# A gated delta-rule kernel: chain matmuls on four array tiles, part of the convolution on TensorE, and a new schedule

## The chip, the cores and the metric

The kernel runs on one core of one Trainium2 chip. The metric is the device time of one execution in microseconds (us). Engines are named as in the profile: PE is TensorE (PEld its weight loads), DVE is VectorE, ACT is ScalarE, POOL is GpSimd, SP is the SyncE queue from which all transfers are issued.

## The reference

There are two parts. The first is a delta-rule recurrence over 768 tokens for 4 batches x 8 heads of width 48, the second a gated convolution block on the result (model width 384, kernel of 5 taps). Cut to what matters:

```python
k_n = k / (norm(k) + 1e-6)
state = zeros(B, H, 48, 48)
for t in range(768):
    y[t] = q[t] @ state
    state += beta[t] * outer(k_n[t], v[t] - k_n[t] @ state)
x = y as [B, S, 384]
gate_pre[s] = sum(conv_w[j] * x[s - 4 + j] for j in range(5))
out = (sigmoid(gate_pre) * (x @ w_val)) @ w_out
```

All values are fp32. The three weights arrive as 64-bit numbers and are turned into fp32 on the chip.

## The kernel before

The tokens are cut into 12 chunks of 64. Within a chunk the recurrence becomes matrix work: with L the masked, scaled matrix of key products of the chunk, one needs the inverse T of a unit triangular 64 x 64 matrix for each of the 32 (batch, head) pairs; then u = T (v - k S), S += k^T u and y = q S + (q k^T masked) u. Heads come in pairs: a state of two heads lies in partitions 0 to 47 and 64 to 111.

Two chunks form a group; there are six groups. The work of a group (`prep`):

- `gram` (L455, or `gram0` L465 for group 0): key and query products, through PSUM into GL by ACT. Group 1 to 5 multiply against block-diagonal keys that are loaded a second time (KBD).
- `diag` (L473, L474) and a 32 x 32 transpose (L478) put the diagonal 32 x 32 blocks of all heads along the free axis, so that DVE can invert them all at once, one partition per row of work. `coef` (L414 to L443) makes the norms by a root iteration.
- The inverse of 32 x 32 blocks: `row` up to 8 (L498, L500), `mergez8` and `merget8` to 16 (L508 to L523), `zmul`, `zred`, `tmul`, `tred` to 32 (L527 to L547). The largest multiplies of the last stage run on POOL (buffers D and PR2), the others on DVE. Two transposes (L552, L554) bring the blocks back.
- `lev1` and `lev2` (L564, L585) join two 32-blocks to a 64-block on PE in 32 x 32 array tiles; ACT copies around them fill BD (`bdcopy` L575).
- `vscale` (L449, POOL) scales the values, `att` (L682, POOL) masks the query products into AQ.

The work of a chunk (`chain`) is done in two halves of 8 head pairs: `emul` (v - kS, as one matmul with the identity stacked under the keys), `umul` (L713), `smul` (L725, L727, accumulated in PSUM), `ymul` (L739, L741), each with an ACT copy out of PSUM. y comes out feature-major; a copy and twelve small SP transfers per chunk (X<-YS) put it into the layout of the second part.

The second part of a chunk (`moe`): for each of three blocks of 128 features, the five taps on [128, 4 x 64] tiles (one ACT copy, `tap` L783 on DVE, one product on ACT added by POOL, L790), the sigmoid (L793), `val` (L798, PE), `gate` (L802, DVE); then `outp` (L809), `oevac` and four stores.

No order is written by hand. Each piece is put into a planner (`Plan`) with an engine, a cost in us and its inputs and outputs; the planner simulates the engines with these costs, a rank (longest path plus a table of biases, BIAS), and gives one order of emission. It also inserts matmuls on zeros (`keep_warm`, L853) where it finds PE idle or thinly loaded.

Of the kernel before, what the change touches and what calls it, by code (L numbers as in the profile page):

```python
# [27 lines left out]
BIAS = {
    'GVH': 49.4, 'GVL': 430.5, 'LB': -960.7, 'LF': 103.3, 'LK': 1063.7, 'LQ': 47.2, 'LV': -635.0, 'Lk0K': 76.9,
    'Lk0Q': -227.5, 'Lkt': 472.7, 'Lo': 12.9, 'Lw': 61.8, 'Lx': 463.6, 'WH': 5.2, 'WL': -222.6, 'XL': 23.3,  # L30
    'att': -654.8, 'bdcopy': 453.2, 'blankB': -14.6, 'blankK': -5.4, 'blankQ': 209.3, 'blankU': -168.4, 'coef': -53.2,
    'conv': -269.0, 'cscale': -35.7, 'diag': -136.2, 'eevac': -29.7, 'emul': -281.2, 'eye': -11.2, 'eyes': 10.6,
    'f64c': 43.2, 'f64cj': 4.7, 'f64cl': 14.4, 'f64o': 61.4, 'f64oj': -34.2, 'f64ol': -83.4, 'f64v': -24.1,
    'f64vl': -54.5, 'fill': 2.2, 'gate': 102.4, 'gevac': -110.2, 'gevac0': 63.3, 'gram': -91.8, 'lev1': -38.0,
    'lev2': 175.8, 'masks': -18.5, 'merget8': 176.4, 'mergez8': -6.7, 'norm_red': -132.3, 'norm_sq': 5.7,
    'outp': 647.7, 'sevac': 334.2, 'sig': -447.3, 'smul': 978.1, 'tap': -856.6, 'tap_product': -1442.2,
    'tap_sum': 526.0, 'tevac': -12.4, 'tmul': -23.0, 'trans_in': 80.0, 'trans_out': 92.7, 'tred': 22.8,
    'uevac': 251.2, 'umul': 622.2, 'val': -383.5, 'vscale': -451.5, 'yevac': 75.3, 'ymul': -21.4, 'zevac': 7.1,
    'zmul': -1217.5, 'zred': -24.9, ('GVH', 0): -59.0, ('GVH', 1): -430.0, ('GVH', 5): 228.9, ('GVL', 1): 101.2,
# [5 lines left out]
    ('att', 0): -27.8, ('att', 1): 1.5, ('att', 5): 6.3, ('bdcopy', 0): 29.7, ('bdcopy', 1): -449.2,  # L45
    ('bdcopy', 5): -329.1, ('blankB', 0): 39.8, ('blankK', 0): -125.7, ('blankQ', 0): 8.4, ('blankU', 0): 68.6,
    ('coef', 0): 14.0, ('coef', 1): 141.0, ('coef', 5): 81.4, ('conv', 0): -53.4, ('conv', 1): -178.5,
    ('conv', 5): 33.1, ('cscale', 0): 4.7, ('cscale', 1): 12.2, ('cscale', 5): 15.9, ('diag', 0): 23.4,
    ('diag', 5): 333.9, ('eevac', 0): 15.5, ('eevac', 1): 80.1, ('eevac', 5): -272.3, ('emul', 1): -1.5,
    ('emul', 5): -5.0, ('eye', 0): 64.3, ('eyes', 0): -3.8, ('f64c', 0): 269.1, ('f64cj', 0): -81.2,  # L50
    ('f64cl', 0): -55.7, ('f64o', 0): -13.4, ('f64oj', 0): -87.5, ('f64ol', 0): 82.9, ('f64vj', 0): 372.9,
    ('f64vl', 0): -98.5, ('fill', 0): -18.9, ('gate', 1): -126.5, ('gate', 5): 236.8, ('gevac', 1): -23.1,
    ('gevac', 5): -92.7, ('gevac0', 0): -365.9, ('gram', 1): -331.6, ('gram', 5): -0.7, ('gram0', 0): 27.8,
    ('halo', 0): 15.7, ('halo', 1): -217.4, ('halo', 5): -331.7, ('lev1', 0): 101.2, ('lev1', 1): 149.0,
    ('lev1', 5): 88.8, ('lev2', 0): 4.1, ('lev2', 1): -57.3, ('lev2', 5): 32.6, ('masks', 0): 209.6,
    ('merget8', 0): 210.5, ('merget8', 1): 72.8, ('merget8', 5): 0.3, ('mergez8', 0): -5.5, ('mergez8', 1): 49.0,
    ('mergez8', 5): 281.0, ('norm_red', 0): -83.0, ('norm_sq', 0): -51.1, ('oevac', 0): -199.0, ('oevac', 1): 169.8,
    ('oevac', 5): -211.1, ('outp', 0): -232.0, ('outp', 1): 40.4, ('row', 0): 14.6, ('sevac', 0): -94.5,
    ('sevac', 1): -307.3, ('sevac', 5): -11.7, ('sig', 0): 5.8, ('sig', 1): -5.8, ('sig', 5): 354.3,
    ('smul', 0): -154.9, ('smul', 1): 128.2, ('smul', 5): -91.0, ('tap', 0): -120.7, ('tap', 1): 22.3,  # L60
    ('tap', 5): 46.7, ('tap_product', 0): -49.4, ('tap_product', 1): -8.8, ('tap_product', 5): 227.5,
    ('tap_sum', 0): -106.3, ('tap_sum', 1): 160.8, ('tap_sum', 5): -86.9, ('tevac', 0): -222.2, ('tevac', 1): -300.8,
    ('tevac', 5): 27.0, ('tmul', 0): -55.3, ('tmul', 1): 203.6, ('tmul', 5): -0.8, ('trans_in', 0): -3.8,
    ('trans_in', 1): -3.0, ('trans_in', 5): -27.1, ('trans_out', 5): 52.7, ('tred', 0): -66.1, ('tred', 1): 89.7,
    ('tred', 5): -16.7, ('uevac', 0): 113.1, ('uevac', 1): 29.9, ('uevac', 5): -10.0, ('umul', 0): -192.2,
    ('umul', 1): -4.4, ('umul', 5): 78.7, ('val', 0): -30.2, ('val', 1): -4.4, ('val', 5): -12.8,
    ('vscale', 0): -102.0, ('vscale', 5): 87.3, ('yevac', 0): 9.1, ('yevac', 1): 136.9, ('yevac', 5): 24.2,
    ('ymul', 0): -3.0, ('ymul', 1): -22.7, ('zevac', 1): 187.4, ('zevac', 5): -1.7, ('zmul', 1): -228.0,
    ('zmul', 5): 72.0, ('zred', 1): 74.8, ('zred', 5): -18.6,
# [11 lines left out]
class Plan:  # L81

    HOP = {"PE": 0.2, "ACT": 0.2, "DVE": 0.12, "POOL": 0.15, "SP": 1.6}  # L90

    def __init__(self, slots, bias):
        self.bias, self.part, self.kinds = bias, 0, []
        self.ops, self.writer, self.readers, self.slots = [], {}, {}, dict(slots)
        self.load = {}

    def pe(self, t, cost, cols):


        part = 0.0  # L100
        while part < 1.0:
            k = int(t / TICK + 1e-9)
            rate = (1.0 if self.load.get(k - 1, 0.0) >= TICK_COLS else 0.5) / cost
            dt = min((1.0 - part) / rate, TICK * (k + 1) - t)
            self.load[k] = self.load.get(k, 0.0) + cols * dt * rate
            part, t = part + dt * rate + 1e-9, t + dt
        return t

    def add(self, eng, cost, fn, args=(), r=(), w=(), take=None, give=None, cols=0, kind=None):
# [818 lines left out]
```

## Time and profile before

| what | value |
|---|---|
| three runs | 412.46 us median (411.55 to 415.64) |
| profiled execution, span | 416.2 us |
| mean granted TensorE clock | 0.881 |
| PE, PEld | 352.4 us, 297.6 us busy |
| DVE, ACT, POOL | 324.6, 233.7, 172.4 us busy |
| PE instructions | 5836 matmuls, 5836 weight loads |
| filler matmuls (L853) | 416 of these, 62.6 us |
| moved by transfers | 45.31 MB, 109 GB/s |

A group line of the profile reads: line, engine, operation, output<-inputs, shapes, count, then busy us, mean ns of one, and the idle time before them with what ended it. The mean of one matmul contains its way through the array, so the busy us divided by the count, or the distance of the starts, is what one costs in a row of many. A windows line reads: stretch, its length, then busy us (and instructions) of PE, PEld, DVE, ACT and POOL, granted clock, DMA share, GB/s.

### The profile page before, as it was taken

How to read it: one execution, taken by the hardware profiler on the slowest of the kernel's cores; microseconds unless marked ns; L12 is line 12 of the kernel's file. 1: busy time of each engine (PE TensorE's matmuls, PEld its weight loads, DVE VectorE, ACT ScalarE, POOL GpSimd, SP SyncE). 2: the span in 40 equal slices, each digit the busy share in tenths (PEclk: the TensorE clock that was granted, in tenths of full speed). 3: DMA queues.
4: the chain of work that ended last, by engine and by line, in shares of the span. 5: the costliest groups of instructions: out<-in, count | busy, mean ns of one | idle time of the engine just before them, and what ended most of it. 6: DMA issues, size and time to landing. Idle time of an engine off the chain costs nothing.

```text
span 416.2 us, 13720 instructions
## 1 busy us (share of the span) xinstructions
PE 352.4 (85%) x5836; PEld 297.6 (71%) x5836; DVE 324.6 (78%) x576; ACT 233.7 (56%) x509; POOL 172.4 (41%) x138
## 2 busy tenths in 40 slices
PE   8849967997499969989798999597599793999995
PEld 6849967886398738767586877476578593878883
DVE  5689999998894998988988379989587999320550
ACT  8403327966386636957377765353777364876420
POOL 4263650837802727505663233557023477100200
...
GB/s 222 166 251 198 157 183 50 145 151 192 52 151 116 142 14 157 104 122 139 154 106 157 128 130 142 106 61 131 49 2 79 78 114 24 2 41 13 48 39 38
DMA packets 59805, 45.31 MB, mean 109 GB/s; under 512 B 44576, under 2 KB 47776, under 8 KB 59744
## 3 DMA queue, kind: packets, MB, share of 16 engines
...
q8 instruction: 46, 0.75, 0.8%
q14 instruction: 15, 0.12, 0.1%
...
## 4 chain that ended last, share of the span: by engine, by line
PE 52%; DVE 21%; DMA 11%; issue 6%; ACT 4%; SPq 3%; POOL 2%; DVEq 0%; POOLq 0%; ACTq 0%
PE gram L455 9%; PE SPS L853 9%; PE val L798 9%; PE out L809 8%; DVE GT L783 6%; PE u L713 4%; SPq L304 3%; DVE TTR L552 2%; DMA GL<-in_kq_dram 2%; PE SPS L725 2%; DMA AQ<-in_conv_w_dram 2%; PE z L564 2%; DVE TT__85 L547 2%; PE gram L465 2%; DVE PR L508 2%
## 5 line engine op out<-in xcount | busy, mean ns | idle before, releaser
L783 DVE SCALAR_TENSOR_TENSOR GT<-X,CW,GT 128x256 f32<-128x256 f32 x111 | 73.1, 684 | 12.9 <-POOL GT L790 12.2
L790 POOL TENSOR_TENSOR GT<-GT,TP 128x256 f32<-128x256 f32 x33 | 27.0, 817 | 97.7 <-ACT TP L299 97.4
L853 PE MATMUL SPS<-ZW 128*128 128x128 f32 x416 | 62.6, 309 | 0.0
L853 PEld LDWEIGHTS SPS<-ZW 128*128 128x128 f32 x416 | 58.5, 220 | 2.7 <-issue 1.0
L798 PE MATMUL val<-X,WV 128*128 128x256 f32 x216 | 58.9, 415 | 1.0 <-ACT BD L299 1.0
L809 PE MATMUL out<-WO,GT 128*128 128x384 f32 x144 | 52.1, 511 | 6.8 <-DVE GT L802 6.7
L455 PE MATMUL gram<-KQ,KBD 96*128 96x128 f32 x320 | 54.5, 331 | 0.8 <-DMA KQ<-in_kq_dram 0.8
L455 PEld LDWEIGHTS gram<-KQ,KBD 96*128 96x128 f32 x320 | 49.0, 237 | 2.3 <-ACT BD L299 0.9
L798 PEld LDWEIGHTS val<-X,WV 128*128 128x128 f32 x216 | 41.2, 203 | 7.6 <-ACT BD L299 1.1
L802 DVE TENSOR_TENSOR GT<-val,GT 128x256 f32<-128x256 f32 x36 | 15.0, 420 | 39.4 <-PE val L798 32.7
L575 ACT ACTIVATE BD<-TTR 32x512 f32<-32x512 f32 x48 | 30.1, 628 | 27.2 <-DVE TTR L552 26.7
L809 PEld LDWEIGHTS out<-WO,GT 128*128 128x128 f32 x144 | 27.4, 198 | 24.6 <-DVE GT L802 7.7
L449 POOL TENSOR_TENSOR US<-VT,NRM 64x768 f32<-64x768 f32 x24 | 36.4, 1516 | 19.7 <-DMA VT<-in_vt_dram 10.7
L299 ACT ACTIVATE GL<-gram 128x512 f32<-128x512 f32 x48 | 27.9, 594 | 23.4 <-PE gram L455 15.9
L793 ACT ACTIVATE GT<-GT 128x256 f32<-128x256 f32 x36 | 14.7, 415 | 43.4 <-DVE GT L783 43.1
L564 PE MATMUL z<-TTR,GL 32*32 32x32 f32 x768 | 12.0, 210 | 29.8 <-DVE TTR L552 21.6
L682 POOL TENSOR_SCALAR_AFFINE_SELECT AQ<-GL 64x1024 f32<-64x1024 f32 x24 | 28.7, 1195 | 15.4 <-PE y L739 8.9
L564 PEld LDWEIGHTS z<-TTR,GL 32*32 32x32 f32 x768 | 9.6, 123 | 34.0 <-DVE TTR L552 15.5
L713 PEld LDWEIGHTS u<-VT,BD 128*64 128x64 f32 x704 | 26.4, 157 | 9.5 <-ACT BD L299 4.5
L713 PE MATMUL u<-VT,BD 128*64 128x48 f32 x704 | 29.0, 242 | 4.5 <-ACT BD L299 3.6
L739 PE MATMUL y<-AQ,US 112*64 112x64 f32 x384 | 28.2, 226 | 1.8 <-ACT X L299 1.8
L299 ACT ACTIVATE OS<-out 128x384 f32<-128x384 f32 x24 | 11.8, 490 | 30.4 <-PE out L809 26.7
...
## 6 DMA issues: line engine op xcount, KB each, us to landing
...
```

Source lines behind the costliest of these rows:

```text
L299: A.activation(out=out, in_=in_, func=AF.Copy, **kw)
L449: G.tensor_tensor(out=USV[(2 * g + c) % 3][r, a], in0=VT[c][r].rearrange("p (h n) d -> p h n d", h=2), in1=n.unsqueeze(3).to_broadcast([64 ...
L455: PE.matmul(p[:, 128 * j:128 * (j + 1)], KBD[h % 2][:, j, :], KQ[h % 2][:, j, :], start=True, stop=True)
L564: PE.matmul(p[to:to + 32, x:x + 32], GL[r + 32:r + 64, u, 0:32], TTR[r + 32:r + 64, u, :], start=True, stop=True, tile_position=(r + 32, to))
L575: A.activation(out=BD[c][q:q + 32, :, q:q + 32], in_=TTR[q:q + 32, u0:u0 + NP, :], func=AF.Copy)
L682: G.affine_select(out=AQ[c][r0:r0 + 64, :, j, :], in_=GL[r0:r0 + 64, c * NP:(c + 1) * NP, 64:128], pattern=[[0, NP], [1, C]], compare_op=A ...
L713: PE.matmul(p[64 * a:64 * a + 64, D * j:D * j + D], BD[c][:, h * HB + j, 64 * a:64 * a + 64], VT[c][:, h * HB + j, :] if ch else us[:, a, ...
L739: PE.matmul(p[0:64, C * j:C * j + C], US[ch % 3][0:112, 0, h, D * j:D * j + 64], AQ[c][0:112, pp, 0, :], start=True, stop=True)
L783: eng.scalar_tensor_tensor(out=GT[m], in0=x[:, m, :, k:k + C], scalar=CW[:, m, k:k + 1], in1=GT[m], op0=ALU.mult, op1=ALU.add)
L798: PE.matmul(p[:, 0:B * C].rearrange("p (b t) -> p b t", t=C), WV[:, k, 128 * m:128 * m + 128], xs[:, k], start=(k == 0), stop=(k == NKT - 1))
L809: PE.matmul(bank["o", ch, i][:, 0:DM], GT[k][:, 2 * i:2 * i + 2, :].rearrange("p b t -> p (b t)"), WO[:, k, :], start=(k == 0), stop=(k == ...
L853: PE.matmul(SPS[0][:, 384:512], ZW, ZW, start=False, stop=True, skip_group_check=True)
```

## The change

The kernel is rewritten around the same algorithm.

- **Pairing.** Partitions 0 to 63 and 64 to 127 now hold tokens of different batches (two streams t, two halves r). Every step of the chain is 32 matmuls of 48 columns, each on one 64 x 64 tile of the array: four tiles in turn (`STREAMS`) in `estep`, `qstep`, `sstep`, `ystep`, two in `ustep`. The subtraction of the values is a DVE operation (`esum`); the part of y from the state (`qstep`) is a step of its own that is accumulated in PSUM with `ystep`.
- **One gram.** Keys and queries of a chunk come in one load KQ (two transfers of 480 KB). `gram` makes 32-token blocks on 64 x 32 tiles, 64 matmuls of 96 columns per chunk; ACT copies the key blocks (`gk`), DVE multiplies the query blocks with a mask (`ga`). `att`, `diag`, KBD and KQ0 go.
- **Inverse.** The 8 and 16 stages are as before. In groups 1 to 5 all multiplies of the last stage are on DVE. In group 0 (`FAST`) the 16 to 32 stage is done by PE and ACT instead (`pack`, `trans_x`, `split`, `p1`, `wsum`, `p2`, `p3`). `bd0`, `zevac`, `tevac` copy on ACT.
- **Values** are scaled on ACT, head by head (16 copies of 48 columns per chunk).
- **y** is token-major; `flip` transposes it on PE against an identity, ACT copies it into X. The twelve transfers go.
- **Taps.** Three of five taps are matmuls with diagonal weights (`conv`, 9 matmuls of 256 columns per chunk), the other two stay on DVE, the first of them reading PSUM. The ACT copy and the POOL addition go.
- **Banks.** PSUM is two banks for the states and six that any piece may take.
- **Schedule.** New costs, ranks and biases in the planner, and a term by which PE gets at most 256 instructions in 3.6 us. Filler is placed by the same kind of rule.

The core of the diff, with the parts that do this (removed functions are named above):

```diff
+SUPPLY = 3.6
+BLOCK = 256
-DENSE = (6.722264986890762e+22, 1800.0, 1300.0)
+DENSE = 600.0
...
+    STREAMS = ((0, 0), (1, 1), (0, 1), (1, 0))
+    def gram(c, i, part):
+        x = KQ[c % NKQ]
+        for j in range(4):
+            h = 4 * i + j
+            for k in range(2):
+                for r, t in STREAMS:
+                    q = 64 * t + 32 * k
...
+                    PE.matmul(o, w, y, start=True, stop=True, tile_position=(64 * r, q))
...
+        if g in FAST:
+            for b in range(2):
+                add("ACT", 0.5, pack, (b,), r=["TT"], w=["PR"])
+            add("DVE", 0.63, trans_x, w=["PR"])
+            add("ACT", 1.15, split, (1,), r=["PR", "MHI"], w=["RH"])
+            add("ACT", 1.15, split, (0,), r=["PR", "TRQ"], w=["TZ"])
...
+        else:
+            for kb in range(4):
+                add("DVE", 0.06 + 64 * (16 - 4 * kb) / 960.0, zmul, (kb,), r=["TL", "TT"], w=["PR"])
+                add("DVE", 0.07 + 64 * (16 - 4 * kb) / 960.0, zred, (kb,), r=["PR"], w=["ZT"])
...
+        def estep():
+            for h in range(H):
+                for r, t in STREAMS:
+                    PE.matmul(bank("e", c, r)[64 * t:64 * t + C, D * h:D * h + D], x[64 * r:64 * r + D, t ^ r, h, 2 * T:4 * T],
+                              sp[64 * r:64 * r + D, t ^ r, h, :], start=True, stop=True, tile_position=(64 * r, 64 * t))
+        def esum(r):
+            V.tensor_tensor(out=ES[:, r], in0=vw(bank("e", c, r)), in1=vn[:, r], op=ALU.subtract)
+        def ustep():
+            for h in range(H):
+                for r in range(2):
+                    for t in (0, 64):
+                        PE.matmul(bank("u", c, r)[t:t + C, D * h:D * h + D], bd[t:t + C, u0 + 8 * r + h, :],
+                                  (ES if c else vn)[t:t + C, r, h, :], start=True, stop=True, tile_position=(t, t))
+        def sstep():
+            for h in range(H):
+                for r, t in STREAMS:
+                    PE.matmul(SPS[t ^ r][64 * r:64 * r + D, D * h:D * h + D], kt_[64 * t:64 * t + C, r, h, :],
+                              us[64 * t:64 * t + C, r, h, :], start=False, stop=True, skip_group_check=True,
+                              tile_position=(64 * t, 64 * r))
...
+        def flip(r):
+            p = bank("x", c, r)
+            for i in range(NKX):
+                PE.transpose(p[:, 128 * i:128 * i + 128], YS[r][c % 2][:, 128 * i:128 * i + 128], EYE)
...
         def conv(m):
-            copy(A, GT[m], x[:, m, :, 0:C], scale=CW[:, m, 0:1])
+            p = bank("c", c, m)[:, 0:B * C].rearrange("p (b t) -> p b t", t=C)
+            for k in range(nt):
+                PE.matmul(p, CD[:, m, k], x[:, m, :, k:k + C], start=(k == 0), stop=(k == nt - 1))
+        def tap(m, k):
+            V.scalar_tensor_tensor(out=GT[m], in0=x[:, m, :, k:k + C], scalar=CW[:, m, k:k + 1],
+                                   in1=csum(m) if k == nt else GT[m], op0=ALU.mult, op1=ALU.add)
```

More of the change, by code (lines that the diff above doesn't have):

```diff
@@ L17 @@
 B, H, S, D = 4, 8, 768, 48
-C = 64
-NG = S // (2 * C)
-NP = 16
+T = 32
+C = 2 * T
+NC = S // C
+NG = NC // 2
 NU = 32
-HB = 8
-QB = 4
+KW = 5 * T
 DM = H * D
-NKT = DM // 128
+NKX = DM // 128
 KS = 5
-WAIT = {"PE": (0, 0), "ACT": (0.25, 0.5), "DVE": (0, 0), "POOL": (0.4, 0.8), "SP": (0.3, 0)}
+NBANK = 6
 BIAS = {
[L29 to L39, printed above, removed]
[5 rows of a table removed]
[L45 to L69, printed above, removed]
-}
@@ L90, with __init__, add @@
     HOP = {"PE": 0.2, "ACT": 0.2, "DVE": 0.12, "POOL": 0.15, "SP": 1.6}
[L92 to L109, printed above, removed]
+    def __init__(self, bias):
+        self.bias, self.part = bias, 0
+        self.ops, self.kinds, self.writer, self.readers = [], [], {}, {}
+        self.bank = {}
+    def add(self, eng, cost, fn, args=(), r=(), w=(), take=(), give=(), cols=0, size=0, kind=None):
         n = len(self.ops)
@@ L207, in forward @@
                 done = free[e] + self.HOP[e]
-            if give:
-                slots[give].append(done)
+            for key in give:
+                banks.append((done, self.where[key]))
             ready[e].remove(n)
@@ L215, in forward @@
                     ready[ops[u][0]].append(u)
+        self.span = max(free.values())
         return start, fill
@@ new lines, with bank, copy @@
+    MHI = sb.tile([128, 1], F32, name="MHI")
+    M0 = sb.tile([128, 1], F32, name="M0")
+    MLO = TRQ[:, 16:17]
+    ZW = sb.tile([128, 128], F32, name="ZW")
+    SPS = [ps.tile([128, 512], F32, name=f"SPS{i}") for i in range(2)]
+    PB = [ps.tile([128, 512], F32, name=f"PB{i}") for i in range(NBANK)]
+    plan = Plan(BIAS)
+    add = plan.add
+    def bank(*key):
+        return PB[plan.where[key]]
+    dma = lambda kb: kb / 230.0
+    def copy(out, in_, **kw):
+        A.activation(out=out, in_=in_, func=AF.Copy, **kw)
@@ new lines, in trans_x, with split, p1 @@
+        def trans_x():
+            V.transpose(out=TX, in_=XL)
+        def split(hi):
+            if hi:
+                copy(RH, TX.rearrange("p j u -> p u j"), scale=MHI[:, 0:1])
+            else:
+                copy(TZ[:, :, 0:16], TX.rearrange("p j u -> p u j"), scale=MLO)
+        def p1(i):
+            for j in range(16):
+                for q in (0, 64, 32, 96):
+                    PE.matmul(bank("w", g, i)[q:q + 32, 16 * j:16 * j + 16], GD[gb][q:q + 32, 16 * i + j, T:],
+                              RH[q:q + 32, 16 * i + j, :], start=True, stop=True, tile_position=(q, q))
@@ L840 @@
-    plan.add("SP", dma(98), load, (BE, beta), w=["BE"], kind="LB")
-    for i in range(1 + 2 * NKT):
-        plan_weights(i)
+            copy(OS[2 * (c % 2) + i], bank("o", c, i)[:, 0:DM])
+        X_ = [("X", c % 3, 0), ("X", c % 3, 1)]
+        if not last:
+            add("POOL", 0.3, halo, r=X_, w=[("Xh", (c + 1) % 3)])
+        for m in range(NKX):
+            gt = ("GT", c % 2, m)
+            add("PE", 0.47 * nt, conv, (m,), cols=512 * nt, size=4 * nt, r=X_ + [("Xh", c % 3), ("CD", m)], w=[("cp", c, m)],
+                take=[("c", c, m)])
+            for k in range(nt, KS):
+                add("DVE", 0.4, tap, (m, k), r=X_ + [("Xh", c % 3), "CW"] + ([("cp", c, m)] if k == nt else []), w=[gt],
+                    give=[("c", c, m)] if k == nt else ())
+            add("ACT", 0.36, sig, (m,), r=[("cp", c, m)] if nt == KS else [], w=[gt], give=[("c", c, m)] if nt == KS else ())
+            add("PE", 1.3, val, (m,), cols=1536, r=X_ + [("W", i) for i in range(1, NKX + 1)], w=[("vp", c, m)],
+                take=[("v", c, m)], size=12)
+            add("DVE", 0.34, gate, (m,), r=[("vp", c, m)], w=[gt], give=[("v", c, m)])
```

1003 lines of the change are left out of this document (500 added, 503 removed), and 15 rows, old and new, of the table BIAS.

## The prediction

> **What bounds the kernel now.** I read the busy shares first, then the chain, the stretches of 10 us, and the waits.
>
> ```profile
> span 416.2 us, 13720 instructions
> PE 352.4 (85%) x5836; PEld 297.6 (71%) x5836; DVE 324.6 (78%) x576; ACT 233.7 (56%) x509; POOL 172.4 (41%) x138
> ...
> PE 52%; DVE 21%; DMA 11%; issue 6%; ACT 4%; SPq 3%; POOL 2%; DVEq 0%; POOLq 0%; ACTq 0%
> ...
> L853 PE MATMUL SPS<-ZW 128*128 128x128 f32 x416 | 62.6, 309 | 0.0
> ```
>
> PE looks like the bound, but L853 is the filler that keeps its clock up. Without it PE works 352.4 - 62.6 = 290 us, less than DVE's 324.6. The stretches show who waits:
>
> ```profile
> 100.00:110.00 10.00, 1.60 (x36) 1.22 (x33) 8.61 (x8) 0.89 (x2) 9.26 (x6) 0.64 0.63 117
> 110.00:120.00 10.00, 9.74 (x159) 8.81 (x159) 9.72 (x18) 9.50 (x18) 3.24 (x3) 0.50 0.62 130
> ...
> 340.00:350.00 10.00, 3.26 (x25) 2.96 (x23) 9.89 (x9) 2.08 (x5) 9.85 (x8) 0.93 0.19 33
> ...
> 370.00:380.00 10.00, 9.92 (x287) 8.77 (x275) 1.17 (x3) 6.63 (x18) 0.00 (x0) 1.00 0.11 25
> ```
>
> The columns are PE, PEld, DVE, ACT and POOL busy, granted clock, DMA share. Once per group (at 100, 340) PE starves while DVE and POOL finish the block inverse, and at 110 the clock it then gets is 0.50. After 350 the last inverse is done, DVE has 1.17 of 10 us to do and PE alone works off what is left.
>
> ```profile
> PE z L564 <- DVE TTR L552: 21.6, 3, 8.2
> ```
>
> So DVE's inverses set the pace up to 350, PE the last 66 us. The profiled execution (416.2 us) lies just above the three runs (411.55 to 415.64, median 412.46): I count 0.99 of the span as the time.
>
> **DVE.** Much of its time is waiting beside POOL. These rows are taps without and with a POOL multiply (263.27 to 267.78) beside them, and the same L540 multiply both ways:
>
> ```profile
> 150.42 1.26 DVE L783 SCALAR_TENSOR_TENSOR GT<-X,CW,GT 128x256 f32<-128x256 f32 x3
> 263.83 5.02 DVE L783 SCALAR_TENSOR_TENSOR GT<-X,CW,GT 128x256 f32<-128x256 f32 x4
> ```
> ```profile
> 265.23 2.55 POOL L527 TENSOR_TENSOR D<-TLP,TT__85 128x1024 f32<-128x1024 f32 x1
> ```
> ```profile
> 55.57 1.04 DVE L540 TENSOR_TENSOR PR<-ZT,TT__85 128x512 f32<-128x512 f32 x1
> ...
> 57.51 1.86 DVE L540 TENSOR_TENSOR PR<-ZT,TT__85 128x768 f32<-128x768 f32 x1
> ```
> ```profile
> 101.67 2.44 DVE L540 TENSOR_TENSOR PR<-ZT,TT__85 128x512 f32<-128x512 f32 x1
> ```
>
> 0.42 us a tap alone, 1.25 beside POOL; 1.04 against 2.44. The change empties POOL (only halo, weights and masks stay), so the short values hold. The other terms:
>
> ```profile
> L783 DVE SCALAR_TENSOR_TENSOR GT<-X,CW,GT 128x256 f32<-128x256 f32 x111 | 73.1, 684 | 12.9 <-POOL GT L790 12.2
> L802 DVE TENSOR_TENSOR GT<-val,GT 128x256 f32<-128x256 f32 x36 | 15.0, 420 | 39.4 <-PE val L798 32.7 <-ACT BD L299 5.6 <-ACT ZS L299 1.1
> L474 DVE SCALAR_TENSOR_TENSOR D<-GL,M,D 128x512 f32<-128x512 f32 x12 | 11.6, 967 | 0.4
> L473 DVE TENSOR_SCALAR D<-GL,M 128x512 f32<-128x512 f32 x12 | 8.5, 709 | 11.2 <-ACT GL L299 11.2
> L534 DVE TENSOR_REDUCE ZT<-D 128x64 f32<-128x1024 f32 x6 | 7.3, 1212 | 1.0 <-POOL D L527 1.0
> ```
>
> - Taps: 111 become 12 x 3 x 2 = 72 at 0.42 = 30: -43. The two diagonal passes (L473, L474) go: -20.
> - Group 0's second merge goes to PE and ACT, with its two transposes: multiplies and reduces of 256 to 1024 columns by the short rows 12, transposes 4, less 1 or 2 for what comes instead: -15.
> - In groups 1 to 5 the multiplies that POOL did come to DVE: 1.2 and 0.95 (as long as a reduce of that size), 1.86, and 2.4 by extension: 6.4 x 5 = +32. What stays is freed of POOL: L540 alone 1.4 x 5; with the smaller merges I take -15 (0 at worst).
> - Added: 48 masked products (ga) of L802's form, 0.42: +20; 22 subtractions of 384 columns (esum), 0.55 (L802 and 128 columns more): +12. In all 324.6 - 43 - 20 - 15 + 32 - 15 + 32 = 296.
>
> **PE.** Costs per call, from the chain (calls in order) and the timeline:
>
> ```profile
> 65.16 1.08 PE z L564 x64
> ...
> 305.74 1.49 PE val L798 x6
> 307.23 1.07 PE u L713 x32
> 308.30 4.07 PE out L809 x12
> ...
> 392.07 1.30 PE val L798 x6
> ```
> ```profile
> 166.22 0.20 PE L725 MATMUL SPS<-US,KT 64*48 64x48 f32 x1
> ...
> 166.85 0.20 PE L725 MATMUL SPS<-US,KT 64*48 64x48 f32 x1
> ```
> ```profile
> 172.66 0.45 PE L564 MATMUL z<-TTR,GL 32*32 32x32 f32 x32
> 173.04 1.16 PE L853 MATMUL SPS<-ZW 128*128 128x128 f32 x8
> ```
>
> Every fp32 matmul is two records (val: 108 in the code, 216 in the profile). 256 columns take 217 to 248 ns a record, so 0.85 ns a column. Alone, 48 columns would take 41 ns and 32 columns 27. But the two tiles of L725/L727 (row halves 0 and 64, opposite column halves) come as a pair every 45 ns (15 pairs from 166.22 to 166.85), and the 32 x 32 tiles of z every 12 ns (32 in 0.38 us). Tiles do overlap, by two and by more.
>
> Per 64-token chunk, after:
> - conv, new: 9 matmuls, 18 records, 3.9 to 4.5, take 4.2. val as now 4.2, outp 4.1.
> - estep, qstep, sstep, ystep: 64 records each on four tiles. Between z's 12 ns (0.76 us) and the pair's 22.5 (1.44); four tiles in the time of the pair is 0.72. I take 0.8, the nearer being z, which also alternates tiles: 3.2.
> - ustep uses two diagonal tiles: 64 x 22.5 ns = 1.4 (2.1 at today's u rate).
> - gram: 128 records of 96 columns, 82 ns per four: 2.6 (1.5 at z's rate, 5.2 by pairs). lev1, lev2: 128 records at 12 to 17 ns: 1.9. flip: 6 transposes of 128 columns: 1.3 (0.65 if one record each).
>
> Sum 23.1; 12 chunks 277, and some 12 for group 0's p1 to p3 and its split gram: 289 us. PE's own work is therefore the same 290 as now: the taps put on it eat what the tiles give. The gain must come from no longer starving and from needing less filler.
>
> **ACT** loses the conv copies and inverse copies and gets xevac, vscale and bd0: per chunk about 10 copies of 384 columns, 3 sigmoids, 4 gram copies, 5 inverse copies, 16 small scalings, some 15 us: 180 in all, under 233.7, hidden behind PE. **SP** loses 72 transfers of y and most key and query loads; I cost this at nothing outside the start and the end, where it is counted below.
>
> **Start and end.**
>
> ```profile
> 8.27 0.84 ACT L407 ACTIVATE D<-KT 128x768 f32<-128x768 f32 x1 [0.96 <-DMA KT<-in_kt_dram]
> ...
> 22.66 2.11 DVE L478 STREAM_TRANSPOSE TLP<-D 128x1024 f32<-128x1024 f32 x1
> ```
> ```profile
> 63.09 1.92 DVE L552 STREAM_TRANSPOSE TTR<-TT__85 128x1024 f32<-128x1024 f32 x1
> ```
> ```profile
> 76.49 2.29 PE L713 MATMUL u<-US,BD 128*64 128x48 f32 x64
> ```
> ```profile
> 377.70 10.95 SPq L304 DMA_DIRECT2D X<-YS  x12
> ```
>
> Now the first u starts at 76.49. After: first keys by 8 (as KT lands now), gram and copy to 11, transpose, norm and scaling to 17, the 8 and 16 merges 9 to 26, group 0's short cut (pack, transpose, two splits, p1, p2, copy) 8, the two levels 6, that is 40, and half of the 12 us of weight conversion in DVE's way: 45. At the end the 11 us of y transfers become flip and xevac, about 2 us.
>
> **Sum.** At 45 us PE has done 22 of its 289. The 267 left run at 90%: 45 + 297 + 4 for the last copies and transfers = 346 by the span, **343 us** as time. DVE alone would allow 10 + 296/0.95 + 9 = 331, so PE is the later, by little. The 90% is a choice (97% would give 322, 82% 372): esum now sits on DVE, in order behind operations of up to 2.1 us; ustep waits for it, and sstep and the next chunk's estep behind that. qstep, conv and val of the chunk before cover it when the order has them there. Uncovered, 11 chunks x 2 us is 22 us, which is most of the 10%.
>
> **Rivals.**
> - DVE still paces: the taps keep their 684 ns and the big multiplies their slow form though POOL is empty. Then 324.6 - 24 - 20 - 15 + 45 (the moved multiplies at 9 a group) + 32 = 343, /0.95 + 19 = 380, 376 as time. Against: 150.42 above. 0.15.
> - Four tiles go only by pairs: four steps of 1.44 and gram 5.2 are +5.2 a chunk, 62/0.9 = +69: 412. For it: no row shows four 64 x 64 tiles. Against: z at 12 ns where one alone needs 27. 0.08. The Trainium skill, TensorEngine Tiling (Array Packing), Restrictions and Gotchas, says that different row tiles cannot access one PSUM bank at the same time. sstep and ystep here send two row tiles to one bank each; by that rule only these two double: 12 x 1.3/0.9 = 17 more, 360. The trace disagrees: L725 and L727 write one bank from row tiles 0 and 64, and a pair takes 45 ns, not 82.
> - Slower: instructions come too slowly.
>
> ```profile
> q8 instruction: 46, 0.75, 0.8%
> ```
> ```profile
> 376.00:381.00 5.00, 4.92 (x161) 4.75 (x157) 0.38 (x1) 2.78 (x7) 0.00 (x0) 1.00 0.05 10
> ```
>
> 46 transfers of 0.75 MB are 16 KB each, and 11672 PE instructions / 46 = 254 in each. The densest 5 us of PE hold 318, 4.0 us per 256; 370:380 holds 562, 4.55 per 256. After, the small steps of a chunk are 1150 instructions in 9.1 us, 2.0 us per 256, a density that no stretch shows. If a block takes 4.55 and the large matmuls (12.5 us) don't hide it, a chunk takes 20.4 + 12.5 = 33: 45 + 12 x 33 - 10 + 4 = 435, 431 as time. It decides from 31.4 us a chunk, 4.2 us a block. Against: 64 instructions in 0.38 us at z, and conv, val and outp are slow enough to fetch under, if the order mixes them. 0.11. The Trainium skill (Runtime: NRT & Kernel Launch, Instruction fetch mechanics) says that the fetch of 16 KB blocks is hidden behind the issue of instructions; by that this rival falls.
> - Better: everything at its low bound, 20 a chunk at 95%: 45 + 230/0.95 + 4 = 291, 288 as time. 0.08.
>
> **Numbers.** The forecast of 343 (its own range 320 to 368) gets 0.58. Range 304 to 405: outside lie part of the better case, the pairs case and the slower one, 0.2 in all. Faster by over 1%: 0.58 + 0.15 + 0.08 + 0.04 = 0.85; within 1%, about what a measurement can tell here: 0.04; slower 0.11. (Of the pairs case half is counted as faster, half as no change.)
>
> **What would show it.** Right: first u near 45; taps near 420 ns and L540's kind near 1.04 for 512; estep's 64 records in 0.7 to 1.0 us; PE without filler near 290 with a span near 345; y's transfers gone. Wrong: PE idle or small steps stretched with "issue" as the releaser (fetch), steps of 1.4 us (pairs), PE waiting on esum or on the inverse in every chunk (DVE), or first u after 55.

## The result and the profile after

The changed kernel takes 387.42 us (four runs, 384.36 to 389.48) against 412.00 (411.44 to 415.64) for the kernel before: a ratio of 0.939, 95% interval 0.931 to 0.948. The forecast was 343, range 304 to 405: the direction is right, and the gain is 25 us where 69 were forecast. The profiled execution took 386.40, span 384.3.

The page of the changed kernel: span, busy shares, granted clock and DMA share in 40 slices, instruction transfers, chain, costly groups.

```profile
span 384.3 us, 18428 instructions
PE 337.5 (88%) x8436; PEld 275.9 (72%) x8436; DVE 261.2 (68%) x599; ACT 179.1 (47%) x495; POOL 20.3 (5%) x31
...
PEclk9555897576589989669999999999999999999999
DMA  8999143041602074611172272523521210102011
...
q8 instruction: 66, 1.08, 1.3%
...
PE 76%; DVE 13%; issue 9%; ACT 1%; ACTq 0%
...
L859 DVE SCALAR_TENSOR_TENSOR GT<-X,CW,PB 128x256 f32<-128x256 f32 x36 | 17.1, 476 | 35.0 <-PE PB L853 34.8
...
L919 PE MATMUL SPS<-ZW 128*128 128x128 f32 x168 | 26.8, 322 | 2.5 <-issue 2.5
```

DVE fell from 324.6 to 261.2 and POOL from 172.4 to 20.3. The fillers (L919) fell from 62.6 to 26.8. The chain is PE for 76%, and "issue" took 9% of it. Without the fillers and the 3.8 us of L345 (zeros written into the two state banks at the start), PE works 306.9 us (289 forecast). In the other 77.4 us of the span it is idle or works on zeros (346 - 289 = 57 forecast). Stretches show where (columns as in the prediction):

```profile
0.00:20.00 20.00, 9.26 (x315) 6.81 (x318) 4.06 (x24) 5.01 (x11) 0.74 (x6) 0.76 0.95 171
20.00:40.00 20.00, 10.05 (x244) 8.58 (x227) 8.74 (x36) 5.15 (x19) 0.48 (x2) 0.50 0.89 231
...
60.00:80.00 20.00, 13.17 (x654) 12.23 (x655) 19.35 (x52) 14.26 (x38) 4.89 (x4) 0.66 0.18 50
80.00:100.00 20.00, 16.41 (x547) 14.71 (x541) 19.55 (x28) 12.63 (x37) 4.98 (x5) 0.64 0.29 83
100.00:120.00 20.00, 20.00 (x527) 17.10 (x523) 7.59 (x19) 9.67 (x22) 3.19 (x5) 0.76 0.34 72
...
140.00:170.00 30.00, 24.39 (x563) 18.82 (x556) 18.15 (x23) 9.27 (x20) 0.22 (x1) 0.73 0.48 101
170.00:200.00 30.00, 29.92 (x834) 23.85 (x832) 15.71 (x50) 13.34 (x33) 0.22 (x1) 0.98 0.32 63
200.00:230.00 30.00, 29.80 (x598) 23.22 (x595) 29.26 (x52) 14.02 (x49) 0.43 (x1) 1.00 0.41 91
```

From 170 on PE has hardly a gap; 39.5 of its 46.8 us of idle time lie before it. DVE is full at times there too (29.26 of 30 at 200). The start is the place to look. First its waits (total, times, longest), then PE's rows with the wait before them:

```profile
PE PB L461 <- issue: 22.2, 5, 9.6
PE SPS L783 <- issue: 4.1, 3, 1.6
PE PB L627 <- issue: 4.0, 2, 2.2
```
```profile
18.39 0.91 PE L461 MATMUL PB<-BD 48*32 48x64 f32 x42 [9.62 <-issue]
29.01 1.20 PE L461 MATMUL PB<-KQ 48*32 48x96 f32 x44 [7.80 <-issue]
...
60.22 0.60 PE L614 MATMUL PB<-RH,GD 32*32 32x16 f32 x49 [1.95 <-issue]
63.77 1.93 PE L627 MATMUL PB<-WS,TZ 32*32 32x32 f32 x128 [2.21 <-issue]
67.50 0.81 PE L627 MATMUL PB<-WS,TZ 32*32 32x32 f32 x44 [1.80 <-issue]
70.95 0.90 PE L639 MATMUL PB<-TZ,WS 32*32 32x32 f32 x49 [1.53 <-issue]
...
80.89 1.31 PE L774 MATMUL PB<-VN,BD 64*64 64x48 f32 x38
```

The first u (L774) starts at 80.89, not 45. PE stands in the middle of a product, waiting for nothing that the profile shows. After each such wait come 128 matmuls (49 + 79, 128, 44 + 84) with 128 weight loads: one block of 256. In the short inverse (p1 to p3: L614, L627, L639) these blocks start 3.55, 3.73 and 3.45 us apart, with 1.3 to 1.9 us of work each. At 9 and 21 us, with the DMA engines at 0.95 and 0.89 in these stretches, a block took far longer. DVE waits with them, in its order:

```profile
20.02 1.94 DVE L499 STREAM_TRANSPOSE TLP<-GD 128x1024 f32<-128x1024 f32 x1 [14.29 <-ACT GD L338]
30.69 0.42 DVE L471 TENSOR_TENSOR AQ<-PB,MASK 128x256 f32<-128x256 f32 x1 [7.24 <-ACT GD L338]
...
38.34 0.15 DVE L537 TENSOR_TENSOR TT__78<-TT__78,TLP 128x4 f32<-128x4 f32 x1
...
51.52 0.69 DVE L563 TENSOR_REDUCE TT__78<-PR 128x64 f32<-128x512 f32 x1
...
54.34 0.68 DVE L603 STREAM_TRANSPOSE PR<-PR 128x512 f32<-128x512 f32 x1
```

Group 1's masked products (ga, L471) stand between group 0's norm steps; group 0's rows and merges run from L537 at 38.3 to L563's end at 52.2.

### The profile page after: what moved, and what is told of

Same layout as the page of the kernel before. It is cut to its first block, busy times and chain, and to the rows that moved or that the text cites. A ratio compares the mean times of both kernels' runs of the same rounds, so it can differ in the third digit from the quotient of the medians.

```text
span 384.3 us, 18428 instructions
## 1 busy us (share of the span) xinstructions
PE 337.5 (88%) x8436; PEld 275.9 (72%) x8436; DVE 261.2 (68%) x599; ACT 179.1 (47%) x495; POOL 20.3 (5%) x31
## 3 DMA queue, kind: packets, MB, share of 16 engines
q8 instruction: 66, 1.08, 1.3%
## 4 chain that ended last, share of the span: by engine, by line
PE 76%; DVE 13%; issue 9%; ACT 1%; ACTq 0%
PE PB L853 14%; PE PB L876 13%; PE PB L868 13%; PE PB L774 7%; PE PB L461 6%; PE PB L794 3%; PE PB L662 3%; PE PB L653 3%; PE PB L802 3%; PE PB L764 3%; PE SPS L919 2%; PE SPS L783 2%; PE PB L812 2%; DVE PR L580 1%; PE SPS L345 1%
## 5 line engine op out<-in xcount | busy, mean ns | idle before, releaser
L853 PE MATMUL PB<-X,CD 128*128 128x256 f32 x216 | 56.2, 408 | 0.0
L876 PE MATMUL PB<-WO,GT 128*128 128x384 f32 x144 | 53.1, 510 | 0.0
L868 PE MATMUL PB<-X,WV 128*128 128x256 f32 x216 | 52.1, 387 | 0.0
L338 ACT ACTIVATE VN<-VN,NRM 128x48 f32<-128x48 f32 x192 | 44.8, 326 | 8.1 <-DVE NRM L528 8.1
L853 PEld LDWEIGHTS PB<-X,CD 128*128 128x128 f32 x216 | 41.6, 200 | 7.5
L868 PEld LDWEIGHTS PB<-X,WV 128*128 128x128 f32 x216 | 39.5, 190 | 6.0
L461 PE MATMUL PB<-KQ 48*32 48x96 f32 (+2 forms) x1536 | 27.1, 271 | 14.2 <-issue 12.5
L876 PEld LDWEIGHTS PB<-WO,GT 128*128 128x128 f32 x144 | 26.8, 195 | 15.5 <-issue 1.2
L461 PEld LDWEIGHTS PB<-KQ 48*32 48x32 f32 x1536 | 21.6, 117 | 19.9 <-issue 16.2
L471 DVE TENSOR_TENSOR AQ<-PB,MASK 128x256 f32<-128x256 f32 x48 | 18.6, 413 | 24.2 <-ACT GD L338 21.3
L919 PE MATMUL SPS<-ZW 128*128 128x128 f32 x168 | 26.8, 322 | 2.5 <-issue 2.5
L919 PEld LDWEIGHTS SPS<-ZW 128*128 128x128 f32 x168 | 25.0, 232 | 4.5 <-issue 4.1
L774 PEld LDWEIGHTS PB<-ES,BD 64*64 64x64 f32 x704 | 24.6, 151 | 4.0 <-issue 2.3
L774 PE MATMUL PB<-ES,BD 64*64 64x48 f32 x704 | 26.1, 235 | 1.0 <-issue 1.0
L338 ACT ACTIVATE OS<-PB 128x384 f32<-128x384 f32 x24 | 11.6, 488 | 31.7 <-PE PB L876 30.4
L580 DVE TENSOR_TENSOR PR<-ZT,TT__78 128x256 f32<-128x256 f32 (+3 forms) x20 | 26.0, 1302 | 0.4
```

The source lines that it names most:

```text
L338: A.activation(out=out, in_=in_, func=AF.Copy, **kw)
L461: PE.matmul(o, w, y, start=True, stop=True, tile_position=(64 * r, q))
L471: V.tensor_tensor(out=AQ[c % NAQ][:, r, 4 * i:4 * i + 4, :].rearrange("p h (n t) -> p h n t", t=T), in0=gview(c, i, r, part)[:, :, 0:3:2, ...
L580: V.tensor_tensor(out=PR[:, 0:64 * n].rearrange("p (k i j) -> p k i j", k=16, i=4), op=ALU.mult, in0=z16[:, :, 0:n].unsqueeze(2).to_broadc ...
L774: PE.matmul(bank("u", c, r)[t:t + C, D * h:D * h + D], bd[t:t + C, u0 + 8 * r + h, :], (ES if c else vn)[t:t + C, r, h, :], start=True, st ...
L853: PE.matmul(p, CD[:, m, k], x[:, m, :, k:k + C], start=(k == 0), stop=(k == nt - 1))
```

## Experiments

All kernels are the changed one with the edit named. "Order kept" means the planned order of every engine. Ratios are to the kernel before.

**Is the four-tile stage real? (order kept)**

```
-            for h in range(H):
-                for r, t in STREAMS:
+            for h, (r, t) in PAIRS:      # eight heads on tiles (0,0),(1,1), then eight on (0,1),(1,0)
```

> The changed kernel in its order, with the four stages that go over four 64x64 tiles (correction, query, state, local output) issued tile pair by tile pair: first the eight heads on the two diagonal tiles, then the eight on the others, the same 32 matmuls. If four tiles at a time is where these stages gain, each goes from 0.8 to 1.1 us for 64 records to about 2.0 (what the u products take on two tiles), 45 stages by 1 us, on PE, which is over 95 per cent busy: 415 to 430. If two tiles are enough (the stage is bound by the rate at which records are issued, about 17 ns each), it stays within 384 to 392.

409.02 us, 0.989 [0.983, 0.995]. The groups of ystep, estep, qstep and sstep (busy us, mean ns of one), changed kernel and then pairs:

```profile
L802 PE MATMUL PB<-US,AQ 64*64 64x48 f32 x768 | 14.9, 227 | 0.0
L764 PE MATMUL PB<-ST,KQ 48*64 48x48 f32 x704 | 13.6, 223 | 0.2
L794 PE MATMUL PB<-ST,KQ 48*64 48x48 f32 x704 | 13.5, 228 | 0.0
L783 PE MATMUL SPS<-US,KT 64*48 64x48 f32 x704 | 11.9, 216 | 4.1 <-issue 4.1
```
```profile
L803 PE MATMUL PB<-US,AQ 64*64 64x48 f32 x768 | 24.2, 224 | 0.0
L765 PE MATMUL PB<-ST,KQ 48*64 48x48 f32 x704 | 21.2, 221 | 0.1
L795 PE MATMUL PB<-ST,KQ 48*64 48x48 f32 x704 | 20.7, 220 | 0.0
L784 PE MATMUL SPS<-US,KT 64*48 64x48 f32 x704 | 19.5, 219 | 5.7 <-issue 5.7
```

One matmul lasts the same; four tiles hold more of them at once. The four stages go from 53.9 to 85.6 us, +31.7 on PE, and the time by +21.6. So four tiles at a time, against two, are worth nearly as much as the whole gain over the kernel before (25 us). (I had put the time 6 to 21 us too high, with 2.0 us for 64 records in place of 1.81.)

**PE or DVE after the start?** One tap more on DVE, by a re-plan and with the order kept:

```
-TAPS = 3
+TAPS = 2          # e4: planned anew; e9: conv issues two of three, tap(m, 3) does two, order kept
```

> Two taps instead of three on PE, three on DVE. It takes 36 matmuls, 18.7 us, from PE and puts 36 taps, 17 us, on DVE, which is busy 68%. If PE bounds from 110 us on (theory C and part of A): 369 to 378. If DVE or the waits bound: no change or slower, 385 to 395.

> The changed kernel in exactly its planned order with one tap of the convolution taken from PE to DVE: 36 matmuls of about 0.47 us less on PE (17 us), 36 taps of 0.48 us more on DVE (17 us). Theory 'PE paces from the first convolution on, at over 95 per cent busy': 370 to 378. Rival 'DVE paces, or DVE and PE in turn': 384 to 400.

402.22 us (0.979 [0.970, 0.988]) and 395.44 (0.954 [0.941, 0.966]). Though PE lost 36 matmuls, neither is faster: e4 is slower than the changed kernel and slower than I had put it in either case; e9 is 8 us slower by the median, with an interval that overlaps the changed kernel's. With the order kept:

```profile
200.00:230.00 30.00, 25.42 (x509) 19.40 (x510) 29.31 (x56) 13.31 (x45) 0.22 (x1) 1.00 0.32 73
...
320.00:350.00 30.00, 26.37 (x636) 20.94 (x636) 22.32 (x34) 11.71 (x24) 0.22 (x1) 0.89 0.07 16
```

In 200 to 230 PE now idles 4.6 us, at a full DVE. In 320 to 350 it idles 3.6 us with DVE busy 22.3 of 30, so DVE is not the whole of it. "PE paces" (370 to 378) falls; the rival "DVE paces, or DVE and PE in turn" (384 to 400) fits the time, and three taps on PE is no worse a place than two.

**Fillers (order kept, left out).**

```
             if n < 0:
-                keep_warm()
                 continue
```

> The changed kernel in its order without its 42 warming matmuls (168 records, 26.8 us of PE's busy time, most of it before 80 us). If they hold the clock as meant: the granted clock in the first 110 us falls below the 0.50 to 0.97 of the changed kernel's 20 us windows, and 388 to 396. If they stand in PE's way: first u 2 to 5 us earlier, 380 to 386.

392.50 us, 0.956 [0.948, 0.963]; mean granted clock 0.853 for 0.887. (The 168 records are 84 matmuls, at two a matmul, not 42.) Three rows of this run:

```profile
40.00:60.00 20.00, 6.93 (x464) 6.46 (x467) 18.73 (x57) 12.75 (x42) 2.00 (x2) 0.50 0.37 72
260.00:290.00 30.00, 26.82 (x575) 20.50 (x561) 21.98 (x34) 9.09 (x22) 0.45 (x2) 0.83 0.37 84
```
```profile
161.78 1.00 PE L461 MATMUL PB<-KQ 48*32 48x96 f32 x33 [5.04 <-issue]
```

The granted clock fell where most fillers stood (0.50 for 0.97 from 40 to 60 us), and yet the first u came 2.7 us earlier (78.23) and chunk 2's u 2.2 us earlier (133.7 for 135.9). The span is 9 us longer all the same: from chunk 2's u to the end it takes 259.7 us, 248.4 in the changed kernel. There PE's waits for instructions reach 5.04 us (1.80 in the changed kernel), and the clock is 0.83 from 260 to 290 (1.00). So the fillers pay, but not in the start; which of the two costs the time is not shown.

**What holds the start.** First, loads and orders changed at once by new plans (e2: group 1's products after group 0's merges; e3: keys held; both planned anew), and the keys held with all other engines' order kept (e1):

```
+    G.tensor_copy(out=KQ[n[1]][r:r + 1, 0, 0, 0:1], in_=GD[0][r:r + 1, 27, C - 1:C])   # e1; POOL: a key load waits for the K products
```

> The order of PE, DVE and ACT is that of the changed kernel; only the first eight key-and-query loads (3.8 MB) are held on SP until the first K products are copied. Theory A (PE's instruction blocks wait behind these loads): the 9.62 us gap of PE at 8.77 shrinks below 3 us and the first u moves from 80.9 to 62 to 70, the time from 387 to 370 to 377. Theory B (blocks come slowly at the start whatever else is moved): the gap stays above 8 us, the loads are late besides, first u at 85 or later, 390 or more. Theory C (PE's sum is the bound, a shorter start is given back): the gap goes but the time stays at 385 to 389.

> The loads stay early; the schedule puts group 1's gram and masked products behind group 0's 16-merge. Theory A': DVE's norm steps stand in order behind masked products that wait for PE, 7.2 us of it at 23.4 and more at 32 to 38; without them first u moves to 68 to 73 and the time to 375 to 381, while the gap of PE at 8.77 stays above 8 us. Theory C: the time stays at 385 to 389. If the fetch gap is the whole loss at the start, first u stays above 77.

> Key loads held back as in the first run and the schedule made with that, so that group 1's gram also falls behind group 0's inverse. Theory A with A': first u at 52 to 60, time 360 to 368. Theory B: no better than the run with the late gram alone. Theory C: 385 or more.

e1: 385.25 us (0.936 [0.927, 0.946]); e2: 408.72 (0.992 [0.987, 0.997]); e3: 407.07 (0.989 [0.981, 0.997]). The new plans tell little of the start: e3 has its first u at 71.04 and takes longer behind it (chunk 2's u at 138.95, then 267 us to the end), and a new plan orders everything anew, so the cause is not separated. In e1 the wait shrinks:

```profile
9.66 0.68 PE L461 MATMUL PB<-BD 48*32 48x64 f32 x43 [1.48 <-issue]
```

So the 9.62 us came from the loads in front of the block. DVE's first transpose came at 11.05, where I had forecast it. But the first u stayed at 81.51: PE now waited 13.0 us for the keys. Theory C, that the gap goes and the time stays, held.

Then orders changed by hand, everything else in its planned order, and limits on the loads (code shortened; "two loads under way" means that a load is issued only when the one before the previous has landed):

```
e5, e7, e8, e10, e16:  todo = reorder(plan, todo, [(which operations, behind which), ...])
e5 own group first | e7 + group 1's last merge behind chunk 1's correction | e8 + keys late
e10 start ordered by hand | e13 = e10 + two loads under way | e16 = e13, two loads to the end, weights later
e14, e15 (order kept): a load is issued when the one before the previous has landed (start; to the end)
```

> The changed kernel with its planned order kept, except at the start: group 1's eight masked copies go behind group 0's transpose of the inverse, its keys' second product, transpose and norm behind group 0's first product of the short inverse, and the two queries' products of chunks 0 and 1 behind the inverse. Group 1's inverse still stands ahead of chunk 1's first correction on DVE. In the changed kernel the first u starts at 80.9, the second at 101.2, the first convolution at 106.6. Theory 'first u sets the end' (the form of my sum: first u plus 303): first u at 62 to 70, and 365 to 374 in all. Theory 'DVE's queue sets it' (DVE must do both groups' inverses and the weights' conversion, some 75 us without a gap from 20 us on, before chunk 1's correction): first u earlier as well, but second u and first convolution still at 93 to 102, and 378 to 390 in all.

> As the run before, and also the last third of group 1's inverse (the merge of the 16-blocks and the two transposes, about 20 us of DVE) goes behind chunk 1's correction and between chunk 0's taps; its two levels on PE go behind chunk 0's output projection. Theory 'DVE's queue': second u at 76 to 85, first convolution at 80 to 90, and 360 to 372 in all, because from the first convolution on PE has no gaps to give the time back. Rival 'given back': group 1's inverse is then late for chunk 2, or the tuned order downstream is lost, and it stays at 380 to 395.

> As the run before, with the eight query and key loads held back until the first keys' products are copied, so that PE's next instruction block does not stand behind them (9.62 us of idle PE became 1.48 that way, but alone it gained nothing). Theory 'DVE's queue': now DVE's first transpose starts at 11 instead of 20 and all that follows is 6 to 9 us earlier: first u 55 to 62, 350 to 364 in all. Rival 'keys late': the held keys reach group 1's products too late and the gain over the run before is under 3 us.

> The changed kernel's planned order from chunk 0's projections on; the start reordered by hand on what the four runs before it showed. Query and key loads held until the first keys' products are copied, in the order chunk 2, 0, 3, 1; the conversion of the convolution weights, which held DVE 7.07 us in the norm steps, behind the rows; ACT's diagonals and value scalings behind the splits; masked copies of chunks 0, 2, 3 in DVE's gaps; nothing between the first product of the short inverse and the first u on PE (7 runs of 128 records, at 3.6 us a block of 256 instructions 25 us) but these products, and no warming matmuls there; the last third of group 1's inverse behind chunk 1's correction and among chunk 0's taps. Theory 'DVE's queue and the block supply set the start, and from the first convolution on it takes 278 us' (277.8 in the changed kernel, 278.4 with own group first): first product of the short inverse at 31 to 36 (56.3 in the changed kernel), first u at 56 to 62 (80.9), first convolution at 76 to 84 (106.5), and 356 to 366 in all. Rival 'given back': first u comes as early, but the second group's inverse or DVE's work makes the stretch after the first convolution 290 or more, and the time is 372 to 390.

> The run with the start reordered by hand, and each of the first loads of keys, values and weights (up to the first buffer that is loaded twice) issued only when the load before the previous one has landed, by a one-element copy on POOL, so that at most two are under way; the loads' order stays. In the run without this PE waited 7.97 us at 39 and 5.88 us at 48 for instructions while the DMA engines stood at 1.01. Theory 'blocks queue behind the loads': both waits under 3 us, first u at 62 to 68 (74.1 there), and since DVE, which had 32 us of idle time between 20 and 100 there, gets on earlier, 376 to 385 in all. Rival 'the same bytes have to come first anyway': the waits turn into waits for keys, first u at 72 to 76, 386 to 394.

> The changed kernel in exactly its planned order of all engines, with only the limit of two loads under way at the start. Theory 'blocks queue behind the loads': the waits of 9.62 and 7.80 us for instructions among the first keys' products become less than 4 us each, DVE's first transpose starts at 11 to 14 instead of 20.0, and, as DVE's queue from there to chunk 1's correction is about 80 us of work with group 1's keys needed in between, first u at 74 to 80 and 378 to 386 in all. Rival 'the same bytes have to come first anyway' (as when the keys were held back whole, 385.25): 384 to 392.

> The changed kernel in exactly its planned order, and the limit of two loads under way kept for all loads of keys, values and weights to the end, not only at the start. With the limit at the start alone the first convolution came 3.7 us earlier, but PE then waited 5.80 us for instructions at 161, while four key loads of 480 KB were under way (1.80 us there in the changed kernel), and the time was the same. Theory 'blocks queue behind the loads, and that gave it back': this wait falls under 3 us, PE's waits for instructions in all from 36 us to under 28, and 378 to 384. Rival 'given back elsewhere' (keys come too late for their products, or POOL's copies hold the next loads back): 385 to 395.

> The same limit on all loads, with the start reordered by hand as in the run before it with two loads, and the conversions of the six large weights moved behind the short inverse (there one of them held DVE 10.7 us and so PE 14.7 us between the two halves of the short inverse). Theory 'the start is queue and supply': first product of the short inverse at 32 to 35, first u at 58 to 64, first convolution at 82 to 92, and 365 to 378 in all. Rival 'DVE's work is the start, whatever the order' (96 to 98 us of DVE work stand before chunk 2's u in every order so far, and the weights must be converted before chunk 0's taps): first u early, but 380 to 395 in all.

Work taken out, and work doubled (order kept):

```
e17 (e18 with two loads):  zmul, zred, tmul, tred:  if g == 1: return
e19:  p1, p2, p3, lev1, lev2:  for j in TWICE if g == 0 else range(16)
```

> The changed kernel in exactly its planned order, without the 16 DVE instructions that merge group 1's two 16-blocks (left out: these 14 us of DVE work between 74 and 91 us; chunks 2 and 3 then use an incomplete inverse). Nothing has to be done later in their place. Theory 'DVE's amount of work sets when PE's full stretch begins': chunk 1's correction comes about 12 us earlier (u at 88 to 92 instead of 101.2, first convolution at 93 to 98 instead of 106.5) and the time falls by 8 to 12 us, to 375 to 380. Rival 'a later point holds it' (the loads and blocks between 140 and 170, at the end of which every order so far stood within 5 us of the same place): first convolution as early, but 382 to 389 in all.

> The same work left out, with at most two loads under way at the start (alone this brought the first u from 80.9 to 76.4 and the time by nothing). Theory 'DVE's amount of work': 371 to 378, the two gains add. Rival 'a later point': no better than the run before by more than 2 us.

> The changed kernel in its planned order, with every matmul of group 0's short inverse and of its two levels (five products, 896 records) issued twice, the second with the same result: 896 records, or 7 runs of 128 with their weight loads, more on PE before the first u, and no work moved. In the changed kernel these runs begin 3.45 to 3.73 us apart, of which PE is busy 1.9. Theory 'instruction supply sets the start': 3.5 us a run, first u 24 to 26 us later, at 104 to 107; if PE's busy time set it, 13 us, at 93 to 96. What of it reaches the end: all, if the start passes straight through (408 to 414); less than 12 us if a later point has as much slack as the runs that made the start shorter suggest (388 to 398).

Times in us, from the profiled execution except the median; u(0), u(2) are the starts of the u products of chunks 0 and 2:

| run | median | ratio, interval | span | u(0) | u(2) | span - u(2) |
|---|---|---|---|---|---|---|
| changed | 387.42 | 0.939 [0.931, 0.948] | 384.3 | 80.9 | 135.9 | 248.4 |
| e1 | 385.25 | 0.936 [0.927, 0.946] | 382.4 | 81.5 | 133.8 | 248.6 |
| e5 | 393.11 | 0.953 [0.942, 0.965] | 389.7 | 82.7 | 141.7 | 248.0 |
| e7 | 403.31 | 0.978 [0.970, 0.985] | 399.2 | 84.7 | 152.8 | 246.4 |
| e8 | 392.10 | 0.952 [0.943, 0.961] | 389.9 | 75.6 | 143.6 | 246.3 |
| e10 | 391.47 | 0.951 [0.943, 0.959] | 387.9 | 74.1 | 140.9 | 247.0 |
| e13 | 396.61 | 0.962 [0.951, 0.973] | 392.6 | 75.9 | 143.2 | 249.4 |
| e14 | 386.57 | 0.942 [0.932, 0.951] | 385.0 | 76.4 | 133.4 | 251.6 |
| e15 | 385.55 | 0.938 [0.930, 0.947] | 382.7 | 82.5 | 136.6 | 246.1 |
| e16 | 393.32 | 0.955 [0.949, 0.961] | 391.5 | 70.9 | 141.4 | 250.1 |
| e17 | 388.13 | 0.946 [0.941, 0.950] | 387.2 | 83.0 | 137.1 | 250.1 |
| e18 | 384.85 | 0.930 [0.923, 0.936] | 380.9 | 77.4 | 128.7 | 252.2 |
| e19 | 413.41 | 0.999 [0.993, 1.004] | 409.2 | 109.7 | 162.4 | 246.8 |

e17 and e18 leave out group 1's last merge, so they compute less than the kernel must. The last column: from chunk 2's u to the end it takes 246 to 252 us in all of these, which change the work before u(2) or the order of loads. (Where work behind u(2) changes it differs: 259.7 in e12.) A start is worth what it does to u(2), not to u(0).

*The pace.* Doubling 896 records put u(0) 28.8 us later, more than the 25 of the supply theory and twice the 13 of PE's work, and the span 24.9 us. Between the first and the last of these rows lie eight blocks in 29.99 us, 3.75 each on the average (3.46 to 4.55):

```profile
61.87 1.90 PE L616 MATMUL PB<-RH,GD 32*32 32x16 f32 x128 [2.43 <-issue]
...
91.86 0.91 PE L641 MATMUL PB<-TZ,WS 32*32 32x32 f32 x49 [1.50 <-issue]
...
109.71 2.58 PE L776 MATMUL PB<-VN,BD 64*64 64x48 f32 x44
```

The start is on the path, and its small matmuls go at the pace at which instructions come. The granted clock was 0.53 and 0.62 in these stretches of 20 us; no run has the same products at full clock, so its part is not separated.

*Loads in front of blocks.* With two loads under way (e14) the waits of 9.62 and 7.80 became the first two of these, and u(2) came 2.5 us earlier. Later PE waited before one lone filler (third row), which depends on nothing:

```profile
14.01 0.91 PE L461 MATMUL PB<-BD 48*32 48x64 f32 x42 [5.59 <-issue]
20.24 1.20 PE L461 MATMUL PB<-KQ 48*32 48x96 f32 x44 [3.41 <-issue]
...
161.21 0.37 PE L919 MATMUL SPS<-ZW 128*128 128x128 f32 x1 [5.80 <-issue]
```

Keeping the limit to the end (e15) brought that wait to 0.99 us, but the time stayed equal to the changed kernel's within its uncertainty: other waits grew (L627: 5.1 us in place of 4.0; L783: 5.3 in place of 4.1). In e13 the limit did not bring u(0) earlier either (75.9 for e10's 74.1): PE stood 14.71 us for DVE, which itself waited 10.74 us before a weight conversion.

*DVE.* The hand-made orders bring the first product of the short inverse from 56.33 to 33.14 (e16) and u(0) to 70.9, and u(2) to 141.4, later than before. What they moved back, group 1's inverse, weights and masks, is due before u(2), and then DVE is the one that is full (19.33 and 19.17 of 20 us in e16):

```profile
100.00:120.00 20.00, 11.28 (x275) 8.80 (x274) 19.33 (x26) 4.95 (x11) 3.35 (x4) 0.77 0.29 61
120.00:140.00 20.00, 18.80 (x266) 14.27 (x266) 19.17 (x61) 12.46 (x43) 0.52 (x3) 0.98 0.12 31
```

So "given back" was right and "DVE's queue sets it alone" fell: with 14 us of DVE work taken out and nothing moved (e17), u(1) stays at 101.5 and the time is the same. PE's own stream between u(0) and u(2) takes 51 to 57 us in the planned order, and PE is busy for most of it (51.4 of 55.0 us in the changed kernel, 50.4 of 54.1 in e17, where DVE has 9 us less to do). It runs at a granted clock of 0.78 and 0.81; what a full clock would save there is open. That both streams must become shorter together is my conclusion; no run did it. e18, which also limits the loads, is 7.2 us earlier at u(2) and 3.4 in the span; its runs spread from 380.13 to 389.08 and its interval overlaps the changed kernel's, so a gain is not shown. No run here is clearly faster than the changed kernel: e1 and e15, 385.25 and 385.55, lie within its spread.

## Why the prediction was wrong, step by step

- **Failed step: "first u at 45".** It came at 80.9, 36 us late; the span is 38 us longer than forecast. By its parts: first transpose at 20.0 in place of 11 (+9; the block behind the key loads); from there to the first merge, at 38.3, 18.3 us for 6 (+12; ga stands in DVE's order and waits for keys and blocks); merges 13.9 us for 9 (+5; ga among them); short cut and levels, from 52.2 on, 28.7 us for 14 (+15; seven blocks at 3.5 us and more, and a low clock). Less the 5 us that I had for weight conversion (half of 12 would be 6), that is the 36. The parts say where the time lay, not that it returns when one is mended: with the keys held (e1) the first transpose came at 11.05 and u(0) at 81.51. What is shown is the pace: 896 records more put u(0) 28.8 us later and the span 24.9 (e19). The low clock was not in the sum at all: 0.50, 0.66 and 0.64 in three of the five stretches before 100, and chunk 1's u took 3.65 us for its 64 records, 2.07 at full clock.
- **The step behind it was also too simple.** I treated the first u as the point from which PE runs. The runs show chunk 2's u as that point, reached by PE's stream and by two groups of DVE work. That the stretch from the first u to the end came out near the forecast (303.4 us for 301) is luck: PE had 282.1 us of work there where I had 267, and 21.3 us of idle time and filler where I had 34.
- **Rival "instructions come too slowly" was priced for the wrong place.** Its price of 4.55 us a block was too high (3.45 to 3.73 in the short inverse, 3.75 on the average in e19), and I spread it over all chunks. After 170 us PE takes a block of 256 only every 5.8 us on the average (9516 instructions in 214.3 us), since conv, val and outp lie between the small matmuls, and it is busy 97%. Behind two stretches of conv (12 and 6 records) a whole block of small ones goes without a wait:

```profile
173.91 2.21 PE L653 MATMUL PB<-BD,GD 32*32 32x32 f32 x128
```

  Within the short inverse nothing larger lies between them. The Trainium skill (Runtime: NRT & Kernel Launch, Instruction fetch mechanics) says that crossing a block is mostly hidden; the trace agrees after 170 us and disagrees in the start, by 1.5 to 2.2 us a block in the short inverse and 9.62 us behind loads.
- **Right: four tiles at a time.** The chain of the changed kernel:

```profile
109.46 1.09 PE PB L802 x64
...
115.86 0.87 PE SPS L783 x64
...
118.23 1.08 PE PB L764 x64
```

  I took 0.8, so 12.5 ns a record where 14 to 17 were measured, and pairs (e11) take up to 1.81, not 1.44. The Trainium skill (TensorEngine Tiling (Array Packing), Restrictions and Gotchas) would have sstep and ystep, two row tiles in one PSUM bank, go by turns; the trace disagrees, sstep being the shortest of the four.
- **Mis-sized terms of PE**: conv 1.50 us a call and val 1.49 (4.5 a chunk each, 4.2 forecast), outp 2.13 (4.3; 4.1), u 2.0 (1.4), the four stages 4.1 (3.2), gram 1.9 (2.6), levels 2.3 (1.9), flip 0.8 (1.3): 24.3 a chunk, before the low clock. My own terms add up to 22.9, not 23.1, so 287 for the 289 that I wrote; 306.9 were measured.
- **DVE**: taps 476 and 483 ns for 420, ga 413 for 420, and 261 in all for 296. The multiplies moved from POOL cost 28 us for 32. The larger part of the difference is what stayed: without POOL beside it, and with group 0's last merge gone, it fell by 62 us, where I had 15 + 15 (the multiply of 512 columns, 2456 ns in L540 before, takes 1095 in L580). The rival of slow DVE operations fell; e9 shows all the same that one tap more on DVE gains nothing.
- **The 90% was near by luck.** From the first u on PE was busy 286.0 of 303.4 us, 93% without fillers: 97% from 170 us on, and less before. The reason that I gave, PE waiting on esum, does not appear: u (L774) waited 1.0 us in all, for instructions.
- **A misreading of the kernel before.** "Once per group" PE starves, I wrote; the row for L564 names three waits in six groups, 21.6 us.
